# Another order for the value chunks that stay in memory, in a two-layer decode kernel

## The chip, the core and the metric

The kernel runs on one core of one Trainium2 chip. The metric is the device time of one execution in microseconds (us). A kernel is run several times, and its median counts. A profile is one further execution, with the hardware profiler on; its own time is told beside it. Of the engines, PE is the matrix engine (PEld its weight loads), DVE the vector engine, ACT the scalar engine, POOL GpSimd, and SP the engine whose queue issues nearly all loads here.

## What is computed

Two layers, each an attention block over a cached K and V and then a token mixer, for two batches of one token. Both layers read the same cache, so that the second layer needs again what the first one read, with a query that depends on all that came before.

```python
B, Sq, D = 2, 1, 512
Hq, Hkv, Sk, Dh = 32, 8, 32768, 128

def _A_ref(x, k_cache, v_cache, wq, wo):
    q = (x @ wq).reshape(B, Sq, Hq, Dh).transpose(0, 2, 1, 3)
    k = jnp.repeat(k_cache, 4, axis=1); v = jnp.repeat(v_cache, 4, axis=1)
    scores = jnp.einsum("bhqd,bhkd->bhqk", q, k) * (Dh ** -0.5)
    o = jnp.einsum("bhqk,bhkd->bhqd", _softmax(scores), v)
    return o.transpose(0, 2, 1, 3).reshape(B, Sq, Hq * Dh) @ wo

def _B_ref(x, w1, b1, w2, b2):
    u = gelu(jnp.einsum("bsd,sf->bdf", _layernorm(x), w1) + b1)
    return (jnp.einsum("bdf,fs->bds", u, w2) + b2).transpose(0, 2, 1)

x = A_x
for layer in range(2):
    x = x + _A_ref(_layernorm(x), A_k_cache, A_v_cache, A_wq, A_wo)
    x = x + _B_ref(_layernorm(x), B_w1, B_b1, B_w2, B_b2)
```

All is in 32 bits. The K and V of one batch and one KV head are 16.8 MB each; 16 such pairs, read in two layers, are more than a gigabyte, and the kernel's loads are almost that.

## The kernel before

**Units and chunks.** A unit is one (layer, batch, KV head): 32 units, numbered `n` in the order of the list `units`. K and V of a unit are eight chunks each, numbered 0 to 7, of 4096 keys (128 partitions x 4096 elements, 2.1 MB). In the text K3 is K chunk 3 of a unit, V3 the same of V. A chunk is worked in two parts, and a part of a chunk is half a cell (below).

**Per unit.** For K (`k_chunk`, L425) PE multiplies each chunk by the query into one of two score tiles, chunks 0 to 3 into the first and 4 to 7 into the second. Then come the maximum (L440 to L456), the transposed scores in `S[0]` and `S[1]` (L460; `S_89` and `S_90` where instructions are listed) and the exponentials (L465, in place). For V (`v_chunk`, L578) PE multiplies each chunk by its part of `S` (V0 to V3 need `S[0]`, V4 to V7 `S[1]`) and sums all eight in PSUM tile `acc`, with `start` at the first matmul and `stop` at the last. Then `out_0` to `out_2` (L546, L548, L618, L245) take `acc` through the output weights into `rows`. `denominators` (L609) is one product between them.

**Layer changes.** Three units stand out, by their numbers: N1 is the last unit of layer 0 for batch 0, N2 the last of layer 0 for batch 1, and N3 the last that uses kept data. The head of N1 and N2, 7, is the keeper. The units around them are, as (layer, batch, head):

| n | unit | what |
|---|---|---|
| N1 | (0, 0, 7) | keeper, layer 0, batch 0: its K0 to K2 and nearly all of its V stay in memory |
| N1 + 1 | (0, 1, 5) | runs while batch 0 goes through the mixer |
| N1 + 2 | (1, 0, 7) | keeper, layer 1, batch 0: uses up what stayed |
| N1 + 3 = N2 | (0, 1, 7) | keeper, layer 0, batch 1: its K and V stay in turn |
| N1 + 4 | (1, 0, 5) | runs while batch 1 goes through the mixer |
| N1 + 5 = N3 | (1, 1, 7) | keeper, layer 1, batch 1: uses up what stayed |
| N1 + 6 | (1, 1, 5) | the next unit, and so on |

At the end of N1 and N2 the mixer runs at once: `mix_1` (L640) between the last two V chunks, `out_0` to `out_2`, `mix_2` (L664), `hidden_sum` (14 ACT activations at L803 with DVE sums at L820), `mix_3` (L828) and `to_columns` (L311), and from that the query of the next layer (L339, L365).

**Memory.** The tile `mem` has 13 cells of one chunk each and a small rest (numbered 13). Cells 0 to 10 take K and V. The next weights for two heads go to cells 9 and 10 or 11 and 12. Of the keeper, K0 to K2 stay in cells 0 to 2 (`KEPT_K`), V1 to V3 in cells 8 to 10, V5 to V7 in cells 3 to 5 (`KEPT`). V4 stays in part: five of its eight pieces in the rest, two of the other three in two PSUM banks, where DVE copies them (L537), and one is loaded again. V0 is loaded again. While all this stays, only cells 6 and 7 are left for the K and V that pass. There `spread` hands out half cells: the K of N1 + 1 and N1 + 4 goes by loads of 1 MB into the four halves 6.5, 7, 7.5, 6 (cell, or cell and a half), in turn.

**Order.** Everything has a time on a list `stream`: one step is one chunk on PE. An entry is a group of chunks that is loaded by one DMA; the groups of a unit are given by `parts`, and a `key` sorts the groups of K and V of neighbouring units against each other. `stream.sort()` fixes PE's order. The loads (`load`, L139, and `load_weights`, L118) are issued by SP in the same order: at a group's first step its load is put in SP's queue, and there it waits until what it overwrites has been read. A load that waits holds all loads behind it. The smaller work (`max_1`, `exponentials`, `out_0`, `load_weights`, ...) is hung on steps by `at`; times are derived from `k_done` and `v_done`, the step after which a chunk is done, and `kbeg` and `vbeg`, where a unit's K and V begin. `buffer` and `spread` choose the cell that came free longest ago; `PLACE_V` gives two of them by hand.

For N1 and N2 the V groups are, in this order, V0, V1 to V3, V4, V5 to V7. For N1 + 2, `FOLLOWS` has the key of each V chunk: V1, V2, V3 run before K0 of the next unit, V0 behind K0 to K2, V4 and V5, V6 behind K3, V7 behind K5. For N3 the V chunks follow the next unit's K in the plain order of their numbers.

Of the kernel before, what the change touches and what calls it, by code (L numbers as in the profile page):

```python
# [16 lines left out]
NG = 4  # L17
# [7 lines left out]
KEPT_K = {0: 0, 1: 1, 2: 2}  # L25
KEPT = {1: (8, 8), 2: (8, 9), 3: (8, 10), 4: (5, 13), 5: (8, 3), 6: (8, 4), 7: (8, 5)}
RING_CELLS = 11
PLACE_V = {(1, 7): 1, (5, 0): 2}
REST = 5
IN_PSUM = (4, 5, 2)  # L30
KEPT_Q = 4
RESIDENT = (5, 7)
TWO_HEADS = ((0, 1), (2, 3), (4, 6), RESIDENT)
FOLLOWS = (2.2, -0.9, -0.8, -0.7, 3.5, 3.6, 3.7, 5.5)
PIECES = (32, 16, 8, 4, 4)
THIN = 16
QT = 4
# [7 lines left out]
def gqa_mixer_kernel(ctx: ExitStack, tc: tile.TileContext, x, kt, v, wqo, cols, out):  # L45
# [21 lines left out]
    NCH = kt.shape[1] // (CK * DH)  # L67
# [32 lines left out]
    WCELL0, WCELLS = RING * RING, 4  # L100
# [178 lines left out]
    N1 = len(units) - 1  # L279
# [15 lines left out]
    def row_tile():  # L295

        return S[HALVES - 1]
# [22 lines left out]
    def unit_of(n):  # L320

        return units[n]
# [165 lines left out]
    def stays(n, c):  # L488

        quads, cell = KEPT.get(c, (0, 0)) if unit_of(n)[2] == keeper else (0, 0)  # L490
        return quads, mem[:, cell * CK : cell * CK + quads * QT * DH]

    def load_v(n, c, m, limit):
# [73 lines left out]
    def v_chunk(n, c, part):  # L567
        very_last = n == NU - 1 and c == NCH - 1
        vc = v_at[n, c]
        half, i = divmod(c, PACK)  # L570


        a, c2 = divmod(i, PACK // 2)
        quads = JT // QT - (THIN // QT if very_last else 0)
        for q in range(part * NG, min(quads, (part + 1) * NG)):
            g = q % NG
            col = (c2 * (JT // QT) + q) * 32 + a * R * QT
            nc.tensor.matmul(  # L578
                acc[32 * g : 32 * g + R * QT, :],
                S[half][:, col : col + R * QT],  # L580
                vc[q],
                start=(c == (n == N1 + 2) and q < NG),
                stop=(c == NCH - 1 and q >= quads - NG),
            )
# [272 lines left out]
    def parts(n, with_v):  # L857

        m = n + with_v
        if m < N1 or n > N3 and m > N3 + 1:  # L860

            loads = ((0, 4), (4, 2), (6, 2)) if m == NU else ((0, 2), (2, 2), (4, 2), (6, 2)) if m == N3 + 2 else GROUPS
            return [(c, k, NCH) for c, k in loads]
        if not with_v:
            loads = ((0, 3), (3, 1), (4, 2), (6, 2)) if n in (N1, N2) else ((0, 2), (2, 2), (4, 2), (6, 2))
            if n in (N1 + 1, N2 + 1):
                loads = ((0, 2), *((c, 1) for c in range(2, NCH)))
            if n in (N1 + 2, N3):
                loads = [(c, 1) for c in range(NCH)]
        elif n in (N1, N2):  # L870
            loads = ((0, 1), (1, 3), (4, 1), (5, 3))
        elif n in (N1 + 1, N2 + 1):
            loads = [(c, 1) for c in range(NCH)]
        elif n < N1:
            loads = ((0, 2), (2, 2), (4, 2), (6, 2))
        else:
            loads = [(c, 1) for c in range(NCH)]
        return [(c, k, RING) for c, k in loads]

    stream = []  # L880
    for n in range(NU):
        stream += [(n * NCH + c + m - 1, 0, n, c, m, limit) for c, m, limit in parts(n, 0)]
        for c, m, limit in parts(n, 1):
            if n in (N1, N2):
                key = (n + 1) * NCH + 1 + (c + 1) / (2 * NCH)
            elif n in (N1 + 1, N2 + 1):
                key = (n + 1) * NCH - 0.5 + max(c / (2 * NCH) - 0.5, c - 2 + m)
            elif n == N1 + 2:
                key = (n + 1) * NCH + FOLLOWS[c]
            else:  # L890
                key = (n + 1) * NCH + c + m - 1 + (LAG if N1 - 1 <= n <= N3 else 0)
            stream.append((key, 1, n, c, m, limit))
    stream.sort()


    kbeg, k_done, vbeg, v_done, brings, starts, t = {}, {}, {}, {}, [], [], 0
    for _, is_v, n, c, m, _ in stream:
        kept_k = unit_of(n)[2] == keeper and c in KEPT_K
        brings += m * [1 - (stays(n, c)[0] / (JT // QT) if is_v else kept_k) * unit_of(n)[0]]
        (vbeg if is_v else kbeg).setdefault(n, t)  # L900
        starts.append(t)
        for j in range(m):
            t += 1
            (v_done if is_v else k_done)[n, c + j] = t
    done = {}

    def at(time, f, *a, rank=1):
        done.setdefault(time, []).append((rank, f, a))
# [3 lines left out]
    mixed = {}  # L912
    for n in range(NU):
        layer, b, h = unit_of(n)
        kend, vend = k_done[n, NCH - 1], v_done[n, NCH - 1]
        ahead = v_done[n - 1, NCH - 1] if n else 0
        urgent = n in (N1, N2, NU - 1)
        if n:
            if n in (N1 + 2, N2 + 2):
# [58 lines left out]
        if units[n] == lay[layer, b][-1]:  # L978
            key = (layer, b)
            at(vend - 1 if change else vend, mix_1, key)  # L980
            at(vend + (1 if change else 2), take_rows, key, row_tile())
            at(vend + (1 if change else 3), mix_2, key)
            at(vend + (0 if change else 1), gelu_table)
            if change:

                assert k_done[n + 1, NCH - 1] == vend + 6
                at(vend + 1, hidden_sum, key)
                at(vend + 4.5, highest, n + 1, 0)
                at(vend + 5, mix_3, key)
                at(vend + 5.5, to_columns, key)  # L990
                mixed[key] = vend + 6
            else:


                begin = vend + 3
                exps = [k_done[m, NCH - 1] + 2 for m in (n + 1, n + 2)]
                exps += [max(e, v_done[m, NCH - 1] + 4) for e, m in zip(exps, (n, n + 1))]
                when = [w for w in range(begin, begin + FT + 1 + len(exps)) if w not in exps][: FT + 1]
                e = when.pop()
                for f, w in enumerate(when):  # L1000
                    at(w + 1, hidden_out, key, f, rank=0)
                    at(w, hidden_tile, key, f, rank=2)
                at(e, take_rows, key, None, rank=2)
                at(e + 1, mix_4, key)
                if layer + 1 < LAYERS:
                    at(e + 2, to_columns, key)
                    mixed[key] = e + 2

    def book(k, m, time):
        for j in range(2 * k, 2 * k + m):  # L1010
            booked.setdefault(j, []).append(time)

    for t0, (_, is_v, n, c, m, _) in zip(starts, stream):
        if n in (N1, N2) and c in (KEPT if is_v else KEPT_K):
            for j in range(m):
                if is_v:
                    book(KEPT[c + j][1], 2 if KEPT[c + j][0] > QT else 1, t0)
                else:
                    book(KEPT_K[c + j], 2, t0)
    hold(WCELL0, 2, v_done[N1 - 2, NCH - 1] + 3)  # L1020
    first = next(t for t, (*_, n, _, m, limit) in zip(starts, stream) if n > N3 and m == PACK)
    for k in range(0, NCH, PACK):
        book(k, 2 * PACK, first + k)
# [10 lines left out]
    t = 0  # L1034
# [70 lines left out]
```

## Time and profile before

| what | value |
|---|---|
| median of 3 runs | 2502.55 us (2501.7 to 2504.92) |
| the profiled execution's own time | 2499.47 us |
| its span on the core | 2497.7 us |
| HBM bytes read | 1061.72 MB |
| PE busy | 1363.6 us (55%) |
| DVE busy | 240.2 us (10%) |
| ACT busy | 187.7 us (8%) |

The span is the time from the first to the last instruction of the program; what lies around it is 1.8 us in the profiled execution. In rows of instructions the columns are start (us from the span's start), duration (us), engine, line, operation, output<-inputs, shapes, and the number of instructions that are merged in the row; in brackets the idle time of the engine before it and what ended it. `SPq` is SP's queue: its rows are the moments at which a load was issued. A row of a load (`x1, 1024.0 KB, 4.9`) has the number of issues, the size and the time from issue to landing. A row that starts with two times (`1125.00:1150.00`) is a stretch: its length, the busy time of PE, PEld, DVE, ACT and POOL with counts, then the granted clock of PE, the mean busy share of the sixteen DMA engines and the GB/s that they moved. A wait row has the waiting engine, what it waited for, the time in all, how many waits, and the longest.

The profile shows each matmul of 32 bits as two rows (instructions listed from the program show it once).

### The profile page before, as it was taken

The numbers are of one execution on the slowest core, as the hardware profiler recorded it, in microseconds if no ns is written. First come the engines' busy times: TensorE is split into PE (matmuls) and PEld (weight loads), VectorE is DVE, ScalarE is ACT, GpSimd is POOL, SyncE is SP. The second block draws the span as 40 slices with busy tenths as digits, with TensorE's granted clock in tenths as the row PEclk, the third lists the DMA queues.
The fourth block names the chain that finished last, engine by engine and source line by source line (L and its number), as shares of the span: only waits on it lengthen the run. The fifth ranks groups of instructions, "written<-read, shape, count | busy, mean of one in ns | idle before, by whom it ended". The sixth has DMA issues, their size and how long they took to land.

```text
span 2497.7 us, 20458 instructions
## 1 busy us (share of the span) xinstructions
PE 1363.6 (55%) x9270; PEld 369.5 (15%) x9270; DVE 240.2 (10%) x632; ACT 187.7 (8%) x554; POOL 4.9 (0%) x17
## 2 busy tenths in 40 slices
PE   4545445545445545657576666455456464456546
PEld 1111111111111111111121111111111111111112
DVE  1000000000000000003113100000000000010002
ACT  0000000000000000002012000000000000011002
POOL 0000000000000000000000000000000000000000
PEclk8777767877777777778887888777778777777778
DMA  9999999999999999999999999999999999999996
GB/s 421 434 435 427 438 433 431 435 429 435 431 435 434 433 430 430 429 429 385 431 429 402 426 408 435 435 435 433 430 434 434 432 430 432 433 433 435 432 433 282
DMA packets 30336, 1063.04 MB, mean 426 GB/s; under 512 B 3621, under 2 KB 3625, under 8 KB 4522
## 3 DMA queue, kind: packets, MB, share of 16 engines
q1 hardware_dynamic: 29960, 1061.70, 98.8%
q8 instruction: 73, 1.20, 0.2%
q14 instruction: 13, 0.11, 0.0%
q10 hardware_dynamic: 290, 0.04, 0.0%
HBM read 1061.72 MB, written 0.00 MB: 425 GB/s over the span
## 4 chain that ended last, share of the span: by engine, by line
DMA 75%; PE 24%; another core or an unknown queue 0%; issue 0%; DVE 0%; ACT 0%; SPq 0%
DMA mem<-in_v_dram 66%; PE acc L578 19%; DMA mem<-in_kt_dram 9%; PE scores L425 3%; PE small L454 0%; PE small L609 0%; PE bcast L339 0%; PE rows L245 0%; PE small L448 0%; PE kept L760 0%; PE bcast L664 0%; PE bcast L640 0%; DVE S L548 0%; ACT mem L770 0%
## 5 line engine op out<-in xcount | busy, mean ns | idle before, releaser
L425 PE MATMUL scores<-mem,small_sb 128*32 128x512 f32 x4096 | 626.7, 730 | 606.3 <-DMA mem<-in_kt_dram 606.2
L578 PE MATMUL acc<-mem,S 128*16 128x512 f32 x4088 | 601.3, 726 | 474.5 <-DMA mem<-in_v_dram 472.1
L425 PEld LDWEIGHTS scores<-mem,small_sb 128*32 128x32 f32 x4096 | 149.0, 128 | 991.2 <-issue 892.2
L465 ACT ACTIVATE S<-S,small_sb 128x128 f32<-128x128 f32 x240 | 123.4, 518 | 2105.8 <-DVE small_sb L456 1630.1
L578 PEld LDWEIGHTS acc<-mem,S 128*16 128x16 f32 x4088 | 133.3, 110 | 834.2 <-issue 666.8
L440 DVE TENSOR_REDUCE small_sb<-scores 128x1 f32<-128x512 f32 x64 | 44.3, 691 | 846.2 <-PE scores L425 846.2
L460 DVE STREAM_TRANSPOSE S<-scores 128x512 f32<-128x512 f32 x64 | 45.5, 710 | 117.0 <-PE acc L578 117.0
L339 PE MATMUL kept<-mem,small_sb 128*2 128x512 f32 x104 | 51.1, 617 | 1.7 <-DVE small_sb L273 1.7
L245 PE MATMUL rows<-mem,small_sb 128*1 128x512 f32 (+1 forms) x276 | 48.6, 613 | 2.6 <-ACT mem L803 2.4
L465 ACT ACTIVATION_READ_ACCUMULATOR S<-S,small_sb 128x1 f32 x240 | 44.9, 187 | 0.0
L611 DVE RECIPROCAL small_sb<-small 128x4 f32<-128x4 f32 x32 | 5.9, 185 | 317.8 <-PE small L609 317.8
L450 DVE TENSOR_REDUCE small_sb<-small 1x4 f32<-1x128 f32 x32 | 8.9, 278 | 272.4 <-PE small L448 272.4
L620 DVE TENSOR_TENSOR small_sb<-small,small_sb 128x4 f32<-128x4 f32 x31 | 5.1, 164 | 293.8 <-PE small L618 293.8
L548 DVE SCALAR_TENSOR_TENSOR S<-acc,small_sb,S 128x128 f32<-128x128 f32 x93 | 32.6, 351 | 3.3
L803 ACT ACTIVATE S<-bcast,small_sb 128x512 f32<-128x512 f32 x28 | 21.6, 778 | 101.5 <-DVE small_sb L672 99.4
L546 DVE TENSOR_SCALAR S<-acc,small_sb 128x128 f32<-128x128 f32 x31 | 10.9, 350 | 171.0 <-PE acc L578 171.0
L365 PE MATMUL small<-small_sb,mem 2*128 2x2 f32 x112 | 14.7, 248 | 19.3 <-DVE mem L361 19.3
L339 PE MATMUL bcast<-mem,small_sb 128*1 128x512 f32 (+1 forms) x40 | 20.9, 638 | 0.0
L618 PEld LDWEIGHTS small<-small_sb,S 128*128 128x128 f32 x62 | 12.4, 250 | 46.4 <-issue 39.6
L820 DVE SCALAR_TENSOR_TENSOR acc<-S,small_sb,acc 128x512 f32<-128x512 f32 x24 | 18.1, 755 | 2.5
L365 PEld LDWEIGHTS small<-small_sb,mem 2*128 2x128 f32 x112 | 13.5, 186 | 32.0 <-DVE mem L361 29.6
L618 PE MATMUL small<-small_sb,S 128*128 128x4 f32 x62 | 15.1, 314 | 3.2 <-DVE S L548 3.2
(134 smaller groups left out, 266.6 us busy)
## 6 DMA issues: line engine op xcount, KB each, us to landing
mem<-in_kt_dram SPq DMA_DIRECT2D x14, 4096.0 KB, 21.9
mem<-in_v_dram SPq DMA_DIRECT2D x9, 4096.0 KB, 29.1
mem<-in_wqo_dram SPq DMA_DIRECT2D x7, 4096.0 KB, 37.7
mem<-in_kt_dram SPq DMA_DIRECT2D x12, 2048.0 KB, 20.9
mem<-in_v_dram SPq DMA_DIRECT2D x4, 6144.0 KB, 31.7
mem<-in_kt_dram SPq DMA_DIRECT2D x24, 1024.0 KB, 9.6
mem<-in_v_dram SPq DMA_DIRECT2D x11, 2048.0 KB, 20.8
mem<-in_v_dram SPq DMA_DIRECT2D x21, 1024.0 KB, 8.2
```

The costliest lines, as they stand in the source:

```text
L245: nc.tensor.matmul(rows[32 * g : 32 * g + b + 1, :], weights if b else weights[:, 1:], row, start=False, stop=True, skip_group_check=True,)
L339: nc.tensor.matmul(q_ps[n][:m, :], xnT[:, d, b : b + m], wq_at(h)[:, d, :], start=(d == 0), stop=(d == DT - 1),)
L365: nc.tensor.matmul(pt[:, r * m : (r + 1) * m], q_row[n][:m, r * DH : (r + 1) * DH], ident[:m, :m], start=True, stop=True,)
L425: nc.tensor.matmul(sc_ps[n, half][32 * g : 32 * g + 32, :], q, kc[k * NG + g], start=(i == 0 and k == 0), stop=(i == PACK - 1 and k == SUB ...
L440: nc.vector.tensor_reduce(mx[n][:, half : half + 1], sc_ps[n, half], axis=AX.X, op=ALU.max)
L460: nc.vector.transpose(S[half], sc_ps[n, half])
L465: nc.scalar.activation(s[:, :, h], s[:, :, h], AF.Exp, bias=neg[n][:, h : h + 1], scale=SCALE, accum_out=lsum[n][:, half, h : h + 1],)
L548: nc.vector.scalar_tensor_tensor(t, acc[:, k * DH : (k + 1) * DH], mask[:, k : k + 1], t, op0=ALU.mult, op1=ALU.add)
L578: nc.tensor.matmul(acc[32 * g : 32 * g + R * QT, :], S[half][:, col : col + R * QT], vc[q], start=(c == (n == N1 + 2) and q < NG), stop=(c ...
L618: nc.tensor.matmul(po[:, :R], row_tile()[:, :DH], selh, start=True, stop=True)
L803: nc.scalar.activation(hid[key, f], px[key], AF.Gelu_apprx_tanh, bias=shift[key][:, f : f + 1], scale=slope[key][:, f : f + 1],)
L820: nc.vector.scalar_tensor_tensor(h if f == FT - 1 else acc, h, w, acc, op0=ALU.mult, op1=ALU.add)
```

## The change

It changes the order of groups, and no computation.

1. For N1 and N2 the groups are V0, V5 to V7, V1 to V3, V4. Their keys go by place in that list, not by chunk number.
2. For N1 + 2 the six chunks V1, V2, V3, V5, V6, V7 run before K0 of the next unit; V0 and V4 behind K2 and K3 as before.
3. For N3 `FOLLOWS` has a row too: V1, V2, V3 run before K2 of the next unit, V0, V5, V6, V7 behind K3 and V4 behind K5.
4. A unit's end and `acc`'s first and last matmul are taken from the order (`vend_of`, `v_from`, `v_to`) and not from chunk numbers. One place given by hand is dropped; V0 of N3 gets the same cell 2 by the rule.

```diff
-PLACE_V = {(1, 7): 1, (5, 0): 2}
+PLACE_V = {(1, 7): 1}
-FOLLOWS = (2.2, -0.9, -0.8, -0.7, 3.5, 3.6, 3.7, 5.5)
+FOLLOWS = {2: (2.2, -0.9, -0.8, -0.7, 3.5, -0.6, -0.5, -0.4), 5: (3.05, 1.1, 1.2, 1.3, 5.1, 3.1, 3.2, 3.3)}
...
-                start=(c == (n == N1 + 2) and q < NG),
-                stop=(c == NCH - 1 and q >= quads - NG),
+                start=(c == v_from[n] and q < NG),
+                stop=(c == v_to[n] and q >= quads - NG),
...
-            loads = ((0, 1), (1, 3), (4, 1), (5, 3))
+            loads = ((0, 1), (5, 3), (1, 3), (4, 1))
...
-        for c, m, limit in parts(n, 1):
+        for i, (c, m, limit) in enumerate(parts(n, 1)):
             if n in (N1, N2):
-                key = (n + 1) * NCH + 1 + (c + 1) / (2 * NCH)
+                key = (n + 1) * NCH + 1 + (i + 1) / (2 * NCH)
             elif n in (N1 + 1, N2 + 1):
                 key = (n + 1) * NCH - 0.5 + max(c / (2 * NCH) - 0.5, c - 2 + m)
-            elif n == N1 + 2:
-                key = (n + 1) * NCH + FOLLOWS[c]
+            elif n - N1 in FOLLOWS:
+                key = (n + 1) * NCH + FOLLOWS[n - N1][c]
...
+        if is_v:
+            v_from.setdefault(n, c)
+            v_to[n], vend_of[n] = c + m - 1, t + m
...
-        kend, vend = k_done[n, NCH - 1], v_done[n, NCH - 1]
-        ahead = v_done[n - 1, NCH - 1] if n else 0
+        kend, vend = k_done[n, NCH - 1], vend_of[n]
+        ahead = vend_of[n - 1] if n else 0
```

On SP, around the end of N1, the piece of the difference is this (128x4096 is a chunk, 128x12288 three chunks in one load, 128x2560 and 128x1536 the two parts of V4, 128x2048 half chunks of the next unit's K; - is the order before, + the order now):

```order
 L139 DMA mem<-in_kt_dram 128x8192
 L139 DMA mem<-in_v_dram 128x4096
-L139 DMA mem<-in_v_dram 128x12288
+L139 DMA mem<-in_v_dram 128x12288 x2
 L139 DMA mem<-in_v_dram 128x2560
 L139 DMA mem<-in_v_dram 128x1536
-L139 DMA mem<-in_v_dram 128x12288
 L139 DMA mem<-in_kt_dram 128x2048 x12
```

The second load of three chunks moved ahead of V4's two parts, which are now the last of the unit; the same piece stands at N2.

On PE at the same place, before:

```order
L578 MATMUL acc<-mem,S_89 16x512 x16
L609 MATMUL small<-small_sb 128x4
L578 MATMUL acc<-mem,S_89 16x512 x16
L578 MATMUL acc<-mem,S_90 16x512 x24
L640 MATMUL bcast<-small_sb 128x128 x4
L578 MATMUL acc<-mem,S_90 16x512 x8
L425 MATMUL scores<-mem,small_sb 32x512 x4
```

and now (eight matmuls of L578 are one V chunk):

```order
L578 MATMUL acc<-mem,S_89 16x512 x8
L578 MATMUL acc<-mem,S_90 16x512 x8
L609 MATMUL small<-small_sb 128x4
L578 MATMUL acc<-mem,S_90 16x512 x16
L578 MATMUL acc<-mem,S_89 16x512 x24
L640 MATMUL bcast<-small_sb 128x128 x4
L578 MATMUL acc<-mem,S_90 16x512 x8
L425 MATMUL scores<-mem,small_sb 32x512 x4
```

The three chunks that read `S_90` (V5 to V7) moved ahead of those that read `S_89` (V1 to V3); L640 still stands ahead of the unit's last V chunk, which is now V4.

On SP where N3 uses up what stayed (128x8192 is a pair of chunks, 128x512 the piece of V4 that is loaded again, L118 the next weights):

```order
 L139 DMA mem<-in_v_dram 128x4096
 L139 DMA mem<-in_kt_dram 128x4096 x2
+L139 DMA mem<-in_kt_dram 128x8192 x2
+L139 DMA mem<-in_v_dram 128x4096
+L118 DMA mem<-in_wqo_dram 128x8192
 L139 DMA mem<-in_kt_dram 128x8192
-L139 DMA mem<-in_v_dram 128x4096
-L139 DMA mem<-in_kt_dram 128x8192 x2
-L118 DMA mem<-in_wqo_dram 128x8192
 L139 DMA mem<-in_v_dram 128x512
 L139 DMA mem<-in_kt_dram 128x8192 x2
```

V0 of N3 now stands behind the pair K2, K3 of the next unit, and the weights ahead of the pair K4, K5 instead of behind it.

More of the change, by code (lines that the diff above doesn't have):

```diff
@@ L893, in gqa_mixer_kernel @@
     stream.sort()
-    kbeg, k_done, vbeg, v_done, brings, starts, t = {}, {}, {}, {}, [], [], 0
+    kbeg, k_done, vbeg, v_done, vend_of, v_from, v_to, brings, starts, t = {}, {}, {}, {}, {}, {}, {}, [], [], 0
     for _, is_v, n, c, m, _ in stream:
@@ L996, in gqa_mixer_kernel @@
                 exps = [k_done[m, NCH - 1] + 2 for m in (n + 1, n + 2)]
-                exps += [max(e, v_done[m, NCH - 1] + 4) for e, m in zip(exps, (n, n + 1))]
+                exps += [max(e, vend_of[m] + 4) for e, m in zip(exps, (n, n + 1))]
                 when = [w for w in range(begin, begin + FT + 1 + len(exps)) if w not in exps][: FT + 1]
@@ L1019, in gqa_mixer_kernel @@
                     book(KEPT_K[c + j], 2, t0)
-    hold(WCELL0, 2, v_done[N1 - 2, NCH - 1] + 3)
+    hold(WCELL0, 2, vend_of[N1 - 2] + 3)
     first = next(t for t, (*_, n, _, m, limit) in zip(starts, stream) if n > N3 and m == PACK)
```

## The prediction

> **What bounds the kernel now.** I read the head of the page and the chain of waits first, then the busy time by stretches, and last the timelines of PE and of SP's queue where the stretches show a hole.
>
> ```profile
> span 2497.7 us, 20458 instructions
> DMA 75%; PE 24%; another core or an unknown queue 0%; issue 0%; DVE 0%; ACT 0%; SPq 0%
> 1125.00:1150.00 25.00, 15.41 (x114) 4.23 (x110) 1.47 (x3) 0.00 (x0) 0.00 (x0) 0.73 0.92 391
> 1150.00:1175.00 25.00, 17.97 (x107) 3.28 (x99) 16.00 (x29) 12.87 (x17) 0.55 (x1) 0.80 0.92 367
> 1250.00:1275.00 25.00, 22.71 (x177) 5.93 (x170) 2.23 (x5) 0.38 (x2) 0.00 (x0) 0.91 0.99 422
> 1325.00:1350.00 25.00, 14.81 (x112) 4.40 (x116) 4.49 (x13) 0.26 (x1) 0.54 (x1) 0.80 0.91 365
> 1450.00:1475.00 25.00, 14.55 (x116) 4.00 (x112) 2.77 (x5) 0.00 (x0) 0.00 (x0) 0.86 0.88 367
> 1500.00:2300.00 800.00, 423.34 (x2852) 114.88 (x2844) 60.56 (x174) 61.56 (x188) 0.54 (x1) 0.76 1.00 433
> ```
>
> The last three columns of a stretch are granted clock, DMA share and GB/s. The transfers are the bound: over long stretches the sixteen DMA engines are never dry, and 433 GB/s is their rate. An edit that moves no bytes can only win back the time in which they stand dry, and that shows in three places: the first layer change (1125 to 1175, twice 0.92: 0.16 x 25 = 4.0 us), the second (1325 to 1350: 0.09 x 25 = 2.2 us), and the place where the second batch's resident V is used up (1450 to 1475: 0.12 x 25 = 3.0 us). Together 9.2 us of 2498 are the ceiling. At 433 GB/s a chunk (2.097 MB) takes 4.84 us, a half chunk 2.42.
>
> **Why they are dry at a layer change.** While the keeper's K and V stay, the next unit's K has only cells 6 and 7, as four half cells; in the order of their first loads I call them A, B, C, D. A half is loaded again when PE has read it.
>
> ```profile
> 1110.00 1.89 PE L578 MATMUL acc<-mem,S 128*16 128x512 f32 x16
> 1122.98 3.62 PE L578 MATMUL acc<-mem,S 128*16 128x512 f32 x16 [11.09 <-DMA mem<-in_v_dram]
> 1142.51 4.95 PE L578 MATMUL acc<-mem,S 128*16 128x512 f32 x32 [9.59 <-DMA mem<-in_v_dram]
> 1147.40 1.16 PE L640 MATMUL bcast<-small_sb 128*128 128x128 f32 x8
> 1148.48 1.91 PE L578 MATMUL acc<-mem,S 128*16 128x512 f32 x16
> 1150.21 1.04 PE L425 MATMUL scores<-mem,small_sb 128*32 128x512 f32 x8
> ...
> 1132.99 0.33 SPq L139 DMA_DIRECT2D mem<-in_kt_dram  x1
> mem<-in_kt_dram SPq DMA_DIRECT2D x1, 1024.0 KB, 19.4
> 1151.31 0.33 SPq L139 DMA_DIRECT2D mem<-in_kt_dram  x1
> mem<-in_kt_dram SPq DMA_DIRECT2D x1, 1024.0 KB, 4.9
> 1157.26 0.33 SPq L139 DMA_DIRECT2D mem<-in_kt_dram  x1
> mem<-in_kt_dram SPq DMA_DIRECT2D x1, 1024.0 KB, 6.5
> 1158.98 0.33 SPq L139 DMA_DIRECT2D mem<-in_kt_dram  x1
> mem<-in_kt_dram SPq DMA_DIRECT2D x1, 1024.0 KB, 9.7
> ```
>
> Sixteen matmul rows are one V chunk, eight a half chunk of K. V5 to V7 come last and land as one transfer at 1142.5. PE needs 4.89 us for two of them (the first matmuls at a low clock), 1.08 for the mixer's L640 and 1.73 for the third, and reads half A at 1150.21. The last rows are issues on SP's queue, each with its time to landing: D was issued at 1132.99 and landed at 1152.4; the second load of A could go out only at 1151.31, that of C at 1157.26, the third of A at 1158.98. Without a hole A, B, C, D and A would have landed 2.42 us apart, from 1154.8 on, the last at 1164.5. It landed at 1168.7, **4.2 us late**, in agreement with the 4.0 of the shares. PE was late because 6 MB arrived at once at the unit's end.
>
> **The change at the two layer changes.** V5 to V7 take the place of V1 to V3, and V4 comes last, alone. The bytes up to the end of V are the same, so the last V still lands at 1142.5, and V1 to V3 one chunk earlier, at 1137.7. PE then works 4.89 + 1.73 us on three chunks, 1.08 on L640, by when V4 is there, and 1.73 on V4: it reads A at 1147.1 instead of 1150.2, **3.1 us earlier**. Ahead of this nothing gets later. V1 to V3 now wait for V0, whose cell 8 they take; PE had finished V0 by 1111.9, and V5 to V7 are on their way until 1123. DVE's two copies of V4 into PSUM move with V4 and run while PE is still on V1 to V3. What is new is D: its cell holds the end of V4, which is now used last, so D's first load goes out at 1147.1 instead of 1132.99.
>
> The price of a reload is the time from issue to landing of a half that finds the queue nearly empty; the rows show 4.9 and 6.5. D: 1147.1 + 4.9 = 1152.0, before the 1152.4 that it had; with 6.5, 1153.6, 1.2 late. A: 1148.2 + 4.9 = 1153.1, due 1154.8. C: 1154.2 + 4.9 = 1159.1, due 1159.7; with 6.5, 1160.7, inside the 1.2 already lost. So the first change wins 3.0 to 4.2 us; I take 3.6, the middle, since both prices come from this very place. At the second change C's two loads read:
>
> ```profile
> 1303.17 0.43 SPq L139 DMA_DIRECT2D mem<-in_kt_dram  x1
> mem<-in_kt_dram SPq DMA_DIRECT2D x1, 1024.0 KB, 37.8
> 1348.38 0.33 SPq L139 DMA_DIRECT2D mem<-in_kt_dram  x1
> mem<-in_kt_dram SPq DMA_DIRECT2D x1, 1024.0 KB, 4.7
> ```
>
> C landed first at 1341.0 and again at 1353.1; four halves at 2.42 would have made it 1350.7, so 2.4 us were lost. The same 3.1 us leave 0 to 1.3 of that: 1.1 to 2.4 won, taken as 1.8.
>
> The Trainium skill ("DMA: Bandwidth & Descriptors", Anatomy of one DMA — SWDGE (gpsimd) path) gives a transfer, on the GpSimd path, a fixed 2.0 us beside its bytes at 436 GB/s. By that, an estimate, a half would need 4.4 us and the reloads would cost nothing, 4.2 and 2.4 us won; the 4.7 and 4.9 here come near it, the 6.5 does not.
>
> What is late next is the new layer's first V, which PE starts after the mixer and the exponentials. The load that follows into its half A had this long:
>
> ```profile
> mem<-in_v_dram SPq DMA_DIRECT2D x1, 1024.0 KB, 6.0
> ```
>
> If the chain through hidden_sum sets it, which begins behind V's end and so comes 3.1 us earlier, and not the landings, 4.2 earlier, 1.1 us of these 6.0 are gone. 4.9 are left: free at the price 4.9, 1.1 lost at near 6.5. I take 0.3 at each change, 0.6 in all, with 0 and 2.2 as ends.
>
> **The change where V is used up.** For the keeper's layer-1 unit of the first batch six resident V chunks run before K0 to K2 instead of three. The stretch 1250 to 1275 has share 0.99, nothing to win; what it could cost:
>
> ```profile
> 1248.41 6.63 PE L578 MATMUL acc<-mem,S 128*16 128x512 f32 x48 [2.40 <-ACT S L465]
> 1264.85 3.52 PE L425 MATMUL scores<-mem,small_sb 128*32 128x512 f32 x16 [2.18 <-DMA mem<-in_kt_dram]
> 1275.81 0.33 SPq L139 DMA_DIRECT2D mem<-in_kt_dram  x1
> ```
>
> V1 to V3 end at 1255.0. Three more chunks at 1.8 us, then K0 to K2 and V0, four chunks, by 1267.6, then K3, which landed near 1264.8, by 1269.4, against 1268.4. Its cell is now taken by the K issued at 1275.81 before; that slack of 6 us covers it, and without it each us would be one. Zero. For the second batch's unit the next weights wait for the cells of V2 and V3:
>
> ```profile
> SPq L118 <- PE acc L578: 17.6, 1, 17.6
> 1446.67 3.62 PE L578 MATMUL acc<-mem,S 128*16 128x512 f32 x32
> 1461.14 3.61 PE L578 MATMUL acc<-mem,S 128*16 128x512 f32 x32
> ...
> 1446.91 0.33 SPq L139 DMA_DIRECT2D mem<-in_kt_dram  x1
> mem<-in_kt_dram SPq DMA_DIRECT2D x1, 4096.0 KB, 18.9
> 1464.82 0.33 SPq L118 DMA_DIRECT2D mem<-in_wqo_dram  x1
> mem<-in_wqo_dram SPq DMA_DIRECT2D x1, 4096.0 KB, 13.4
> ```
>
> V2 and V3 ran at 1461.14, behind a K pair, and SP held the weights 17.6 us for them with everything else behind. The K pair ahead of the weights landed at 1465.8; two chunks more would be 1475.5; the weights landed at 1478.2, **2.7 us late**. Now V1, V2 and V3 run straight after K0 and K1: 1446.7 + 3 x 1.8 = 1452.1, and 0.3 for a product between. Weights issued at 1452.4 land, by their own 13.4, at 1465.8. The loads before them are one pair fewer than before, so 1465.8 is also when they are due: the hole closes, with nothing to spare. Ends 2.0 (the lead short by 0.7) and 3.0 (the share); I take 2.7. The K pair behind the weights finds its cells free since 1446.7.
>
> **Sum.** 3.6 + 1.8 + 2.7 - 0.6 = 7.5 us off the profiled execution's 2499.47 makes 2492.0. That execution lies 3.1 below the median of the runs, 2502.55, which becomes 2495.0. The ends are 3.0 + 1.1 + 2.0 - 2.2 = 3.9 and 4.2 + 2.4 + 3.0 = 9.6.
>
> **Rivals.** *The ring of four halves stays short*: D waiting for V4 takes the place of A waiting for V7, every reload costs 6.5, the first V loses its 1.1, and the gain is the low end, 3.9: 2498.6. For it speak the 6.5 and the clearances of 0.4 and 0.6 at D and C; against it 4.7 and 4.9. *The hole is the mixer's, not V's*: if the mixer's chain held the ring, only the weights' 2.7 come, 2499.9. Against it: the first reload that came late, A's, waited for PE's V alone. *Slower: V1 to V4 run wholly at the low clock.*
>
> ```profile
> 1140.00:1145.00 5.00, 2.49 (x12) 0.49 (x16) 0.00 (x0) 0.00 (x0) 0.00 (x0) 0.50 0.92 383
> 1145.00:1150.00 5.00, 5.00 (x48) 1.95 (x44) 0.00 (x0) 0.00 (x0) 0.00 (x0) 0.98 0.68 282
> ```
>
> The chunk at 1122.98 took its 3.6 us wholly at the low clock. Four such and L640 at twice its time are 16.4 us, V4 ends at 1154.1, A is read by 1156.2, C, 6.0 behind A and 2.1 more for two slow halves, by 1164.3; with 4.9 it lands at 1169.2 where 1159.7 was due: 9.5 late where 4.2 were, 5.3 worse at each change, 10.6 in all, less 2.7: 2510.4. It decides if the clock is still 0.50 behind the third chunk. The stretches speak against it: 0.50 about 1142.5, 0.98 from 1145. The Trainium skill ("TensorE: Matmul & The Clock Gate", What's actually happening) lets the array run at half rate after an idle window and at full rate after some 3.4 us of work. By that rule, with which these rows agree, four chunks in a row do warm up.
>
> **Chances.** The forecast 0.72, the short ring 0.14, the mixer 0.08, the low clock 0.06. A measurement of this kernel can tell about 0.2%, 5.0 us, from no change: the forecast lies beyond that, the rivals with 3.9 and 2.7 don't. So faster 0.72, same 0.22, slower 0.06. The forecast's own range is 2493 to 2497.5; 2491.5 to 2501 takes in the short ring and the mixer too.
>
> **What would show it.** Right: shares near 1.0 in the stretches around both layer changes and at the weights; half A read about 4.6 us behind V4's landing, where it was 7.7 behind the last V's; the weights out before the K pair that stood ahead of them; the same bytes. Wrong: a share under 0.9 behind V4's end (the short ring), a clock of 0.50 through V1 to V4, or a new hole of over 1 us elsewhere, above all where the new layer's V begins.

## The result, and the profile after

The changed kernel takes 2497.6 us (median of 13 runs, 2495.84 to 2499.63), the kernel before 2502.68 (13 runs on the same chip, 2501.39 to 2505.26). The ratio is 0.9978, 95% interval 0.997 to 0.9987: **5.1 us faster**, by the interval 3.3 to 7.5. Forecast were 2495.0 and 7.5 us. The time is on the predicted side and inside the wide range, 2491.5 to 2501, but 0.1 us above the forecast's own, 2493 to 2497.5; the gain is two thirds of what was computed, and no more than about the 5.0 us that the prediction thought a measurement can tell from nothing. The profiled execution of the changed kernel took 2498.0 us, its span is 2496.2.

First the same stretches as in the prediction, now of the changed kernel (start and end; length; busy time of PE, PEld, DVE, ACT and POOL; granted clock, DMA share, GB/s):

```profile
1125.00:1150.00 25.00, 17.99 (x128) 4.86 (x124) 2.87 (x7) 0.00 (x0) 0.00 (x0) 0.80 0.90 371
1150.00:1175.00 25.00, 17.39 (x100) 3.54 (x100) 15.57 (x29) 12.86 (x17) 1.08 (x2) 0.80 1.00 404
1250.00:1275.00 25.00, 25.00 (x204) 7.02 (x196) 2.83 (x6) 0.50 (x2) 0.00 (x0) 0.98 0.99 422
1325.00:1350.00 25.00, 17.55 (x124) 4.69 (x124) 7.39 (x18) 2.40 (x4) 0.54 (x1) 0.86 0.93 364
1450.00:1475.00 25.00, 12.65 (x114) 3.40 (x114) 2.76 (x5) 0.00 (x0) 0.00 (x0) 0.82 0.98 415
```

The hole at the weights is closed: 0.88 became 0.98, 367 GB/s became 415. The second layer change is almost as it was (0.91 to 0.93, 365 to 364 GB/s). At the first, the hole in the second stretch went (367 to 404 GB/s), and the first stretch moves even less than before (391 to 371): the hole comes earlier, since everything around it does. Stretches that take in the whole of each place, with the first profile of before and then the one of the change, say it more plainly:

```profile
1125.00:1190.00 65.00, 46.93 (x308) 11.83 (x300) 25.65 (x49) 14.13 (x19) 1.09 (x2) 0.82 0.94 386
1325.00:1390.00 65.00, 46.86 (x310) 12.23 (x311) 24.30 (x47) 14.13 (x19) 1.08 (x2) 0.84 0.97 398
1450.00:1500.00 50.00, 30.19 (x203) 8.06 (x203) 4.33 (x10) 0.00 (x0) 0.00 (x0) 0.83 0.95 405
```

```profile
1125.00:1190.00 65.00, 48.16 (x308) 11.75 (x300) 25.58 (x49) 14.12 (x19) 1.08 (x2) 0.84 0.96 387
1325.00:1390.00 65.00, 50.05 (x328) 12.70 (x329) 25.55 (x49) 14.11 (x19) 1.08 (x2) 0.87 0.98 398
1450.00:1500.00 50.00, 33.66 (x249) 9.95 (x253) 6.27 (x16) 0.00 (x0) 0.00 (x0) 0.83 1.00 428
```

23 GB/s more over 50 us are 1.15 MB, at 433 GB/s **2.7 us won at the weights**, exactly the term of the prediction. At the two layer changes the two profiles moved the same bytes in these windows; the landings, at the end of the experiments, tell more.

Why that is, PE and SP's queue show. PE of the changed kernel at the first layer change (start, duration, idle time before in brackets):

```profile
1137.55 7.50 PE L578 MATMUL acc<-mem,S 128*16 128x512 f32 x48 [6.24 <-DMA mem<-in_v_dram]
1144.98 1.16 PE L640 MATMUL bcast<-small_sb 128*128 128x128 f32 x8
1146.07 1.91 PE L578 MATMUL acc<-mem,S 128*16 128x512 f32 x16
1147.79 1.04 PE L425 MATMUL scores<-mem,small_sb 128*32 128x512 f32 x8
...
1152.66 1.12 PE L664 MATMUL bcast<-S,small_sb 128*128 128x512 f32 x2 [0.81 <-DVE S L632]
1153.72 1.92 PE L425 MATMUL scores<-mem,small_sb 128*32 128x512 f32 x16
```

And from SP's timeline and the view of the transfers, each issue with its time to landing: the first load of D, the second loads of A and C, the third of A, and the weights.

```profile
1148.04 0.33 SPq L139 DMA_DIRECT2D mem<-in_kt_dram  x1
mem<-in_kt_dram SPq DMA_DIRECT2D x1, 1024.0 KB, 5.1
1148.90 0.33 SPq L139 DMA_DIRECT2D mem<-in_kt_dram  x1
mem<-in_kt_dram SPq DMA_DIRECT2D x1, 1024.0 KB, 6.8
1154.85 0.33 SPq L139 DMA_DIRECT2D mem<-in_kt_dram  x1
mem<-in_kt_dram SPq DMA_DIRECT2D x1, 1024.0 KB, 6.8
1156.93 0.33 SPq L139 DMA_DIRECT2D mem<-in_kt_dram  x1
mem<-in_kt_dram SPq DMA_DIRECT2D x1, 1024.0 KB, 10.7
...
1452.22 0.33 SPq L118 DMA_DIRECT2D mem<-in_wqo_dram  x1
mem<-in_wqo_dram SPq DMA_DIRECT2D x1, 4096.0 KB, 13.5
```

PE starts V1 to V3 at 1137.55 (computed: 1137.7) and reads half A at 1147.79 (computed: 1147.1; before: 1150.21). Adding issue and time to landing, and beside it the due times of the prediction:

| load | predicted landing | due without a hole | landed | late |
|---|---|---|---|---|
| D, first | 1152.0 to 1153.6 | 1152.4 | 1153.1 | 0.7 |
| A, second | 1153.1 | 1154.8 | 1155.7 | 0.9 |
| C, second | 1159.1 to 1160.7 | 1159.7 | 1161.7 | 2.0 |
| A, third | 1164.5 to 1165.7 | 1164.5 | 1167.6 | 3.1 |
| weights | 1465.8 | 1465.8 | 1465.7 | none |

(D's due time is A's less 2.42.) The third load of A, which came 4.2 us late before, comes 3.1 late now: 1.1 us won where 3.0 to 4.2 were computed. And it did not last: the load behind the new layer's first V, eight halves behind A's third, was issued at 1181.48 and had this long.

```profile
mem<-in_v_dram SPq DMA_DIRECT2D x1, 1024.0 KB, 7.2
```

It landed at 1188.7, where before it had landed at 1188.6 (issued at 1182.58, the prediction's 6.0 us). In this execution the first layer change brought nothing in the end.

### The profile page after: what moved, and what is told of

Same layout as the page of the kernel before. It is cut to its first block, busy times and chain, and to the rows that moved or that the text cites. A ratio compares the mean times of both kernels' runs of the same rounds, so it can differ in the third digit from the quotient of the medians.

```text
span 2496.2 us, 20457 instructions
## 1 busy us (share of the span) xinstructions
PE 1374.8 (55%) x9270; PEld 373.0 (15%) x9270; DVE 240.2 (10%) x632; ACT 187.4 (8%) x554; POOL 4.9 (0%) x17
## 4 chain that ended last, share of the span: by engine, by line
DMA 74%; PE 24%; another core or an unknown queue 0%; issue 0%; DVE 0%; ACT 0%; SPq 0%
DMA mem<-in_v_dram 63%; PE acc L578 19%; DMA mem<-in_kt_dram 12%; PE scores L425 3%; PE small L454 0%; PE small L609 0%; PE rows L245 0%; PE bcast L339 0%; PE small L448 0%; PE kept L760 0%; PE bcast L664 0%; PE bcast L640 0%; DVE S L548 0%; ACT S L465 0%
## 5 line engine op out<-in xcount | busy, mean ns | idle before, releaser
L425 PE MATMUL scores<-mem,small_sb 128*32 128x512 f32 x4096 | 634.8, 739 | 610.0 <-DMA mem<-in_kt_dram 609.9
L578 PE MATMUL acc<-mem,S 128*16 128x512 f32 x4088 | 601.4, 728 | 459.8 <-DMA mem<-in_v_dram 453.4
L578 PEld LDWEIGHTS acc<-mem,S 128*16 128x16 f32 x4088 | 133.1, 110 | 819.9 <-issue 694.1
L440 DVE TENSOR_REDUCE small_sb<-scores 128x1 f32<-128x512 f32 x64 | 44.2, 691 | 813.6 <-PE scores L425 813.6
L245 PE MATMUL rows<-mem,small_sb 128*1 128x512 f32 (+1 forms) x276 | 49.0, 605 | 2.6 <-ACT mem L803 2.4
L448 PE MATMUL small<-small_sb 128*1 128x128 f32 x64 | 16.6, 353 | 1.5 <-DVE small_sb L446 1.3
```

The lines of the kernel that those rows point to most:

```text
L245: nc.tensor.matmul(rows[32 * g : 32 * g + b + 1, :], weights if b else weights[:, 1:], row, start=False, stop=True, skip_group_check=True,)
L425: nc.tensor.matmul(sc_ps[n, half][32 * g : 32 * g + 32, :], q, kc[k * NG + g], start=(i == 0 and k == 0), stop=(i == PACK - 1 and k == SUB ...
L440: nc.vector.tensor_reduce(mx[n][:, half : half + 1], sc_ps[n, half], axis=AX.X, op=ALU.max)
L448: nc.tensor.matmul(pm[:1, :P], mxa, ident, start=True, stop=True)
L578: nc.tensor.matmul(acc[32 * g : 32 * g + R * QT, :], S[half][:, col : col + R * QT], vc[q], start=(c == v_from[n] and q < NG), stop=(c == ...
```

## The experiments

Each row: median, runs, ratio to the kernel before on the same chip with its 95% interval.

| kernel | us | runs | ratio |
|---|---|---|---|
| the change | 2497.6 | 13 | 0.9978 (0.997 to 0.9987) |
| e1, weights' order alone | 2499.97 | 11 | 0.9993 (0.9984 to 1.0002) |
| e2, layer changes and first using-up | 2499.54 | 11 | 0.9989 (0.998 to 0.9998) |
| e3, first using-up alone | 2501.85 | 11 | 1.0002 (0.9993 to 1.001) |
| e5, V5 to V7 last and one by one | 2493.59 | 5 | 0.9965 (0.9952 to 0.9977) |
| e6, V1 to V3 last, as one | 2501.04 | 11 | 0.9997 (0.9988 to 1.0006) |
| e7, mixer behind half D | 2495.72 | 8 | 0.9975 (0.9965 to 0.9985) |
| e8, e5 and e7 together | 2493.86 | 6 | 0.997 (0.9958 to 0.9982) |
| e9, V1 to V3 one by one, V4 last | 2493.0 | 6 | 0.9967 (0.9955 to 0.9979) |

The medians of the kernel before beside these are 2502.35 (e1 to e3, 27 runs), 2502.11 (e5 to e8, 19 runs) and 2502.16 (e9, 10 runs). e4 and e10 are second profiles of the kernels before and after.

**The parts of the change, apart.** Edits against the changed kernel. The order at the layer changes was not run without the first using-up of six chunks; e2 carries both, and e3 the latter alone.

e1:

```diff
-FOLLOWS = {2: (2.2, -0.9, -0.8, -0.7, 3.5, -0.6, -0.5, -0.4), 5: (...)}
+FOLLOWS = {2: (2.2, -0.9, -0.8, -0.7, 3.5, 3.6, 3.7, 5.5), 5: (...)}
-            loads = ((0, 1), (5, 3), (1, 3), (4, 1))
+            loads = ((0, 1), (1, 3), (4, 1), (5, 3))
```

> Only the order at the second using-up is changed (V1 to V3 of N3 ahead of the pair K2, K3; the weights ahead of K4, K5); the layer changes keep V5 to V7 last. Forecast's theory (layer changes 4.8 us, weights 2.7 us): 2.7 us faster, 2500.0. Rival, that the layer changes won nothing in the end and all of the measured 5.1 us lies at the weights: 5 us faster, 2497.6. Both: the weights are issued as soon as V3 is done, and the stretch around them has a share near 1.0.

e2:

```diff
-PLACE_V = {(1, 7): 1}
+PLACE_V = {(1, 7): 1, (5, 0): 2}
-FOLLOWS = {2: (...), 5: (3.05, 1.1, 1.2, 1.3, 5.1, 3.1, 3.2, 3.3)}
+FOLLOWS = {2: (...)}
```

> The new order at both layer changes and the six V chunks ahead of K0 at the first using-up; the second using-up as before, so the weights wait as before. Forecast's theory: 4.8 us faster, 2497.9. Rival (the ring of four halves stays short and gives back at the new layer's first V what was won): 0 to 1 us faster, 2502, with the load behind that first V landing no earlier than before, near 1188.6 us from the start.

e3 is e2 with the old order at the layer changes:

```diff
-            loads = ((0, 1), (5, 3), (1, 3), (4, 1))
+            loads = ((0, 1), (1, 3), (4, 1), (5, 3))
```

> Only the first using-up is changed: six V chunks ahead of K0 to K2. Every theory here has it at nothing: within 1 us of the kernel before, share of the stretch 1250 to 1275 at 0.99 as before.

Against the 2502.35 of before, e1 wins 2.4 us, e2 2.8, e3 0.5 by the medians (by its ratio it loses 0.5: nothing that can be told). In e2 the load behind the new layer's first V landed at 1187.2 and not near the rival's 1188.6. 2.4 and 2.8 make 5.2, the change as a whole won 5.1: the parts add up as far as intervals of some 2 us to either side can show it. The interval of e1 reaches just over 1, so its 2.4 us rest on the stretch from 1450 to 1500 as much as on the times: e1 moved 418 GB/s there and e3, with the old order of the weights, 402; 16 GB/s over 50 us are 1.8 us at 433 GB/s.

**The kernel before, again (e4).**

> The kernel before, unchanged, for a second profile: how far two profiles of one kernel differ at the three holes. If the holes are a property of the order, they are there again with 4.0, 2.2 and 3.0 us within 0.5 us each, and the own time of this execution is nearer to the median 2502.7 than 2499.5 was.

This execution took 2502.93 us, 3.5 more than the first profiled one. Its long stretches:

```profile
1125.00:1190.00 65.00, 47.95 (x308) 12.23 (x300) 25.63 (x49) 14.13 (x19) 1.09 (x2) 0.81 0.92 375
1325.00:1390.00 65.00, 44.95 (x288) 11.50 (x284) 24.38 (x47) 14.13 (x19) 1.08 (x2) 0.84 0.94 388
1450.00:1500.00 50.00, 32.60 (x210) 7.71 (x202) 2.77 (x5) 0.00 (x0) 0.00 (x0) 0.76 0.95 404
```

The weights' hole is the same (404 and 405 GB/s), while the layer changes moved 375 and 388 GB/s where the first profile has 386 and 398. 21 GB/s over 65 us are 3.2 us at 433 GB/s, nearly all of the 3.5 between the two executions. How deep these two holes are differs from one execution to the next, and the first profile had shallow ones: e1 and e3, with the old order there, have 382 and 386, and 383 and 386 GB/s. The prediction's own sum from shares gives 4.5, 3.3 and 2.3 us for e4, where 4.0, 2.2 and 3.0 were expected within 0.5; the last two are further off than that, and the total is 10.0 instead of 9.2.

**Which chunks come last (e6).** The order of the change with V4 ahead of V1 to V3:

```diff
-            loads = ((0, 1), (5, 3), (1, 3), (4, 1))
+            loads = ((0, 1), (5, 3), (4, 1), (1, 3))
```

> Both using-ups as in the change, at the layer changes V0, V5 to V7, V4, V1 to V3: three chunks land together at the end again, only other ones. If what counts is how much lands last: from the first load of A to the third 23.5 us as before the change, and the time is that of the using-up at the weights alone, 2500. If it counts which chunks come last (V1 to V3 read the first half of S): as the change, 2497.6.

2501.04 us: all that the layer changes had won is gone, and a little more than expected. PE at the first layer change:

```profile
1142.65 5.71 PE L578 MATMUL acc<-mem,S 128*16 128x512 f32 x32 [10.37 <-DMA mem<-in_v_dram]
1151.10 1.04 PE L425 MATMUL scores<-mem,small_sb 128*32 128x512 f32 x8
```

Again three chunks land as one at 1142.65 and PE reads A at 1151.10. It is not V1 to V3 against V5 to V7 that counts, it is how much lands last.

**No 6 MB at the end (e5).** The old order of chunks, with V5 to V7 in three loads:

```diff
-            loads = ((0, 1), (5, 3), (1, 3), (4, 1))
+            loads = ((0, 1), (1, 3), (4, 1), (5, 1), (6, 1), (7, 1))
```

> Both using-ups as in the change, but at the layer changes the old order V0, V1 to V3, V4, V5 to V7, with V5, V6, V7 as three loads of one chunk: what lands last is again one chunk, and half D's cell is free early. If what the change left at the layer changes (some 3 us at the first, 2.4 at the second, from the first load of A to the third 22.6 us where 19.4 would be seamless) is D's new wait for V4 (short ring): A to third A about 21 us, and 2 to 3 us faster than the change, 2495. If it is PE's own work between halves B and C (the mixer's products and their waits, 1150.8 to 1153.7): D early brings little, A to third A 22 us or more, within 1 us of the change, 2497.5.

2493.59 us, 8.5 less than before and 4 less than the change, more than either theory had. Here PE keeps up with the landings:

```profile
1142.76 1.91 PE L578 MATMUL acc<-mem,S 128*16 128x512 f32 x16 [0.27 <-DMA mem<-in_v_dram]
1145.25 1.07 PE L425 MATMUL scores<-mem,small_sb 128*32 128x512 f32 x8 [0.58 <-DMA mem<-in_kt_dram]
```

The brackets are what to read: PE waits for V7 and then for half A. Before and in the change the same rows have no bracket, since PE came to them late.

**The mixer's products (e7).** In the change `rows` (L245) and L664 stand ahead of half C, which PE reads at 1153.72, 3.8 us after it landed (1149.9 by the trace). L664 and `hidden_sum` are moved behind half D, at both layer changes; L245 stays:

```diff
-            at(vend + (1 if change else 3), mix_2, key)
+            at(vend + (2 if change else 3), mix_2, key)
-                at(vend + 1, hidden_sum, key)
+                at(vend + 2, hidden_sum, key)
```

> The change, with L664 and hidden_sum put one chunk later, behind halves C and D, at both layer changes. PE reads C some 2 us earlier, without the wait for DVE. If the work between B and C is what keeps the ring short: C's second load goes out 2 us earlier, A to third A 21 us instead of 22.6, and 2 to 3 us faster than the change, 2495; hidden_sum ends 1.6 us later and still before the product behind it. If the ring is short by D: no change, 2497.6.

2495.72 us, 6.4 less than before, where the change won 5.1. PE's three chunks, and then the second load of C and the third of A:

```profile
1137.45 6.69 PE L578 MATMUL acc<-mem,S 128*16 128x512 f32 x48 [6.98 <-DMA mem<-in_v_dram]
...
1151.86 0.33 SPq L139 DMA_DIRECT2D mem<-in_kt_dram  x1
mem<-in_kt_dram SPq DMA_DIRECT2D x1, 1024.0 KB, 7.9
1156.04 0.33 SPq L139 DMA_DIRECT2D mem<-in_kt_dram  x1
mem<-in_kt_dram SPq DMA_DIRECT2D x1, 1024.0 KB, 9.3
```

C's second load goes out 3.0 us earlier than in the change and lands at 1159.8, on time; the third of A at 1165.3, 0.8 late. In this execution PE also took only 6.69 us for V1 to V3, so that a part of these 3.0 us is not the edit's. By the ratios (0.9975 and 0.9978, with wide overlap) e7 can't be told from the change; for it speak four of its eight runs that lie below the fastest of the change's thirteen.

**Both (e8).** e5 and e7 in one kernel.

> Both of the last edits together: single loads at the end and the mixer behind half D. If both causes count, the gains add: A to third A 20 us, 2493. If they are two names of one lateness (PE reads C late), together they bring no more than the better of them.

2493.86 us, no better than e5 alone. The two edits cure the same lateness: where PE keeps up with V, the mixer's place costs nothing.

**D's wait, or the 6 MB (e9).** e5 changed two things against the change: PE is on time, and D's cell is free early, because V4 isn't last. e9 keeps V4 last and splits V1 to V3:

```diff
-            loads = ((0, 1), (5, 3), (1, 3), (4, 1))
+            loads = ((0, 1), (5, 3), (1, 1), (2, 1), (3, 1), (4, 1))
```

> The changed kernel with V1, V2 and V3 in three loads of 2 MB instead of one of 6 MB; the order of the chunks (V0, V5 to V7, V1, V2, V3, V4) and all else as in the change, so that D's cell still waits for V4, which is used last. Theory (PE is late for half A because 6 MB arrive at once): PE takes V1 to V3 as they land, reads A within 0.6 us of its landing and the third load of A lands about 20 to 21 us after the first (22.6 in the change, 19.9 with V5 to V7 in single loads), time about 2494 to 2495. Rival (D, which waits for V4 in this order and not in the order with V5 to V7 last, is what hurts): still 22 us or more, time about 2497 to 2498.

2493.0 us, 9.2 less than before; the rival falls (five of the six runs lie below the fastest of the change's thirteen). PE, then the loads of D, A, C and A again, then the long stretches:

```profile
1141.85 1.91 PE L578 MATMUL acc<-mem,S 128*16 128x512 f32 x16
1144.98 1.06 PE L425 MATMUL scores<-mem,small_sb 128*32 128x512 f32 x8 [1.23 <-DMA mem<-in_kt_dram]
```

```profile
1143.92 0.33 SPq L139 DMA_DIRECT2D mem<-in_kt_dram  x1
mem<-in_kt_dram SPq DMA_DIRECT2D x1, 1024.0 KB, 8.5
1146.11 0.33 SPq L139 DMA_DIRECT2D mem<-in_kt_dram  x1
mem<-in_kt_dram SPq DMA_DIRECT2D x1, 1024.0 KB, 8.8
1153.93 0.33 SPq L139 DMA_DIRECT2D mem<-in_kt_dram  x1
mem<-in_kt_dram SPq DMA_DIRECT2D x1, 1024.0 KB, 5.9
1156.12 0.33 SPq L139 DMA_DIRECT2D mem<-in_kt_dram  x1
mem<-in_kt_dram SPq DMA_DIRECT2D x1, 1024.0 KB, 8.8
```

```profile
1125.00:1190.00 65.00, 49.08 (x316) 11.83 (x308) 25.56 (x49) 14.13 (x19) 1.09 (x2) 0.87 1.00 409
1325.00:1390.00 65.00, 49.44 (x314) 13.14 (x315) 26.20 (x50) 14.13 (x19) 1.08 (x2) 0.89 1.00 414
1450.00:1500.00 50.00, 31.81 (x222) 8.79 (x214) 6.87 (x17) 1.70 (x7) 0.00 (x0) 0.80 0.99 426
```

D still waits for V4, and goes out at 1143.92 when PE has read it. D, A, C and A land at 1152.4, 1154.9, 1159.8 and 1164.9: within 0.4 us the due times of the prediction, 1152.4, 1154.8, 1159.7 and 1164.5. No load is late, and the share is 0.99 to 1.00 at all three places.

**The change, again (e10).**

> The changed kernel as it is, for a second profile. Theory: the second load of C again lands 1 to 3 us behind its due time (first load of A + 14.9 us), A's third load 21 to 23 us behind its first, and the load behind the new layer's first V takes whatever that leaves. Rival: what the first profile showed is one execution's accident, and here the two changes come out seamless, 20 us each, as forecast.

2498.81 us in one execution. PE's three chunks, the second load of C, and the long stretches at the layer changes:

```profile
1137.37 8.08 PE L578 MATMUL acc<-mem,S 128*16 128x512 f32 x48 [7.25 <-DMA mem<-in_v_dram]
...
1155.24 0.33 SPq L139 DMA_DIRECT2D mem<-in_kt_dram  x1
mem<-in_kt_dram SPq DMA_DIRECT2D x1, 1024.0 KB, 6.7
...
1125.00:1190.00 65.00, 48.38 (x308) 11.88 (x300) 25.61 (x49) 14.13 (x19) 1.09 (x2) 0.81 0.94 384
1325.00:1390.00 65.00, 49.27 (x314) 12.60 (x318) 25.63 (x49) 14.13 (x19) 1.08 (x2) 0.84 0.96 392
```

C lands at 1161.9, 2.2 late: the first profile of the change was no accident. Over two profiles each, the layer changes moved 380.5 and 393 GB/s before, 385.5 and 395 after; 7 GB/s over 65 us are 1.1 us at 433 GB/s. With the 2.7 of the weights that is 3.8 of the 5.1 us. These windows cut the rows of loads at fixed times, though, and other profiles have the same orders. The landings need no windows: from half A's first landing to that of the load behind the new layer's first V are sixteen halves of 1 MB, and they took, by issue plus time to landing, at the two layer changes (us):

| order at the layer changes | profile | first | second |
|---|---|---|---|
| old, V5 to V7 last as one | before | 43.6 | 43.2 |
| | e4 | 44.2 | 44.5 |
| | e1 | 43.0 | 44.7 |
| | e3 | 43.1 | 44.3 |
| of the change | change | 43.8 | 41.1 |
| | e10 | 43.1 | 42.7 |
| | e2 | 42.2 | 42.8 |
| V1 to V3 last as one | e6 | 45.7 | 44.9 |
| of the change, mixer behind half D | e7 | 40.4 | 41.2 |
| single loads | e5 | 39.7 | 39.9 |
| | e8 | 39.8 | 39.8 |
| | e9 | 40.3 | 39.7 |

On average the old order takes 43.5 and 44.2, the change's 43.0 and 42.2: 0.4 us won at the first layer change, less than profiles of one order differ, and 2.0 at the second. 2.4 together agree with e2, and with the 2.7 of the weights they make the 5.1.

## Why the prediction was right, and what in it was wrong

*What bounds the kernel, and the ceiling: right.* The transfers are the bound, and the dry time in three places is about all that the orders tried here could win: e9, whose halves land 2.5 us apart at both layer changes, wins 9.2. That this is the ceiling to the tenth is luck: the interval of e9's ratio goes from 5.3 to 11.3 us, and the same sum from e4's shares is 10.0.

*The weights, 2.7: right.* Issued at 1452.22 (computed 1452.4), landed at 1465.7 (1465.8); 2.7 us by the stretch, 2.4 by e1's median, 1.8 by e1's stretch.

*The first using-up, zero: right* (e3).

*The layer changes, 3.6 + 1.8, less 0.6 for the new layer's first V: the mechanism right, the size wrong.* 4.8 us were computed; e2 measured 2.8 by the medians (by its interval 0.5 to 5.0), the rows of landings give 2.4. The second change's 2.0 are near its 1.8 less 0.3; at the first 3.6 less 0.3 were computed, and 0.4 came. What held: V1 to V3 land one chunk earlier, PE comes earlier, D waits for V4 and lands where it was said. Two steps failed, both told here at the first change.

The larger one is **the price of a reload**, "A: 1148.2 + 4.9 = 1153.1, due 1154.8". 4.9 was the time of a half that found the queue nearly empty. A didn't: D had gone out 0.9 us ahead of it, and A took 6.8 us and landed 2.6 behind D. The lines of the prediction already said so, since a half takes 2.42 and D was to land at 1152.0 to 1153.6: A couldn't land before 1154.4 to 1156.0. Each load was priced by itself where the loads stand in a line, so D's lateness is handed to A and to all behind it. That is 0.9 of the 3.1 us by which A's third load came late. The rest came behind A, in a row that was slower than one half in 2.42 us: B landed 2.9 behind A (at 1158.6, where PE reads it), C 3.0 behind B and 2.0 late, where the upper end said 1.0. In e9, where no load ahead was late, the second load of C needed 5.9 us and was on time, though it went out 3.4 us ahead of B's landing and in the change 3.8; so how far ahead C went out does not tell the two apart.

The smaller one is **PE's time for V1 to V3**: 4.89 + 1.73 = 6.62 us were computed, 7.50 and 8.08 measured, and 6.69 in e7. A chunk takes 3.62 us at the low clock (the prediction's row) and about 1.8 at the full one, so the time over 5.4 us is half of the low phase: 4.2 us, 5.4 us and 2.6 us of work at the low clock in otherwise equal rows, where the prediction took 2.6 for granted from one. The rival of the low clock thus came true in a small part: the full clock came during the second chunk of three, and 0.7 to 1.1 us were lost; for its price it would have had to be missing behind the third. The Trainium skill ("TensorE: Matmul & The Clock Gate", What's actually happening) calls this phase some 3.4 us of time and variable from run to run; these rows, at 2.6 to 5.4, lie on both sides of it.

*The new layer's first V, 0.3 us at each change: inside its ends.* From A's third load to the load behind that V the old order took 19.8 to 20.5 us at the first change (20.0 on average), the new one 21.1, 20.3 (e10) and 19.9 (e2): 0.4 more on average, and 1.1 in the change's first profile, where it took back all that A had won.

*The signs.* A share near 1.0 came at the weights (0.98), not around the layer changes (0.90 and 0.93). The first of the signs of being wrong, a share under 0.9 about V4's end, did come: 0.61 from 1145 to 1150, where before it was 0.68.

*The rival of the short ring* described what happened better than the forecast did: reloads at 6.5 and more, and a gain that was cut at the layer changes. Its time, 2498.6, is 1.0 from the measured 2497.6, the forecast's 2.6. But its cause, D that waits for V4, is not the cause: in e9 D waits for V4 as well and nothing is lost. What keeps the ring short is that PE gets 6 MB at once and then stands behind the landings, 2.9 us at half A (landed 1144.9 by the trace, read 1147.79), and 3.8 at C with the mixer's products between. *The rival of the mixer* is wrong as told (e5 and e9 close the holes without touching it), but the mixer's place may be a part of the lateness as long as PE is late: e7's rows of landings are 40.4 and 41.2 us, its times can't be told from the change's, and at the first change its PE was faster too, so this is not shown.

*The offset of 3.1 us* between the profiled execution and the median was the scatter of one execution, as e4 shows: the changed kernel's own profile lies 0.4 us above its median. The forecast of the median is not hurt by it, since the gain was taken off both alike; the holes at the layer changes, though, were read from an execution in which they were shallow, by the rows of landings the second above all (43.2 us, where e4, e1 and e3 have 44.3 to 44.7).

A version faster than both kernels is e9, at 2493.0 us, with e5 beside it at 2493.59: the splitting, in either order of the chunks, closes the holes at both layer changes, 39.7 to 40.3 us for sixteen halves, 2.5 each.

What stays open: why in the change the row behind the dry time is slow, so that C lost 1.1 us on A, and the third load of A a further 1.1 on C, although it went out at 1156.93, 4.7 us ahead of C's landing. It is not told by the shares of the transfers (below), and was not tried apart.

## What to carry to other kernels

A load that waits for its buffer lands no sooner than the load ahead of it plus its own bytes, and is to be priced by the bare time only where the queue is empty; lateness was handed down the line here and not recovered, and behind a dry time the line lost 2.2 us more than that rule says. Where work must keep up with landings so that buffers come free, the size of the last transfer before it counts more than the order of the chunks: three loads of 2 MB in place of one of 6 MB made the change win 9.2 us instead of 5.1. A row of landings, followed to its end, says more than stretches: part of what is won at its head can be lost further back. And a gain that is computed to a few us from one profile needs a second profile of the kernel before: here its holes differed by 11 GB/s over 65 us, 1.7 us, between two executions.

## What the runs showed of the hardware that was not expected

- The busy share of the transfers can be near 1 while less is moved. In the change, two stretches of 5 us, one behind the restart and one at the new layer's first V, have shares of 0.98 and 1.00 and only 333 and 331 GB/s, where 433 is the rate:

```profile
1155.00:1160.00 5.00, 3.06 (x24) 0.34 (x16) 3.14 (x6) 3.48 (x5) 0.54 (x1) 0.90 0.98 333
1180.00:1185.00 5.00, 4.24 (x34) 1.46 (x32) 2.35 (x5) 0.41 (x2) 0.00 (x0) 1.00 1.00 331
```

  The landings bear both out: in the first stretch (1 - 333/433) x 5 = 1.2 us, and C landed 6.0 us behind A where two halves take 4.84; behind the second a load landed 3.7 us behind the one ahead of it (1185.0 and 1188.7). But a low rate over 5 us is no proof either: e9 has 375 and 385 GB/s from 1145 to 1155, at shares of 0.99 and 0.98, while its halves land 2.5 us apart. Which of these is a hole the landings decide.
- The low clock after an idle stretch of 6 to 7 us lasted between 2.6 and 5.4 us of work at the same place (6.69 to 8.08 us for the same 48 rows).
- In a seamless row of halves (e9) the landings from A's second to A's third load are 10.0 us apart, four halves at 2.50, where 433 GB/s would make them 2.42.
